# Lightning attention and MLP on one core: the first two windows opened tile by tile

## The chip, the cores and the metric

The kernel runs on one core of one Trainium2 chip. Its engines work side by side, each through its own list of instructions in the order written: TensorE (PE) multiplies, VectorE (DVE), ScalarE (ACT) and GpSimd (POOL) do elementwise work, SyncE (SP) issues transfers; ACT and POOL issue some too. The metric is the device time of one execution in microseconds; the runs of the kernel before took 214.71, 215.11 and 215.28 us, the median is 215.11.

## The reference

Inputs are q, k, v of shape 4 (batch) x 8 (heads) x 768 (tokens) x 64, and a decay lam per head.

```python
Dmask = np.where(rel >= 0, lam[:, None, None] ** rel[None, :, :], 0.0)
for b in range(nb):                       # blocks of 64 tokens
    intra = np.einsum('bhic,bhjc->bhij', qb, kb) * Dmask[None]
    intra = np.einsum('bhij,bhjd->bhid', intra, vb)
    inter = np.einsum('bhid,bhde->bhie', qb * lam_pow[None], kv_state)
    out[:, :, sl] = intra + inter
    kv_state = lam_block[None, :, None, None] * kv_state + np.einsum('bhsd,bhse->bhde', kb_dec, vb)
...
xn = (x - mu) / np.sqrt(var + 1e-06) * g_ln
ch = np.maximum(xn @ w_ch1, 0.0) @ w_ch2
return (x + ch).astype(np.float32)
```

So: causal linear attention with an exponential decay and a running K·V state, heads put side by side to 512 columns, then a normalised two-layer MLP (512 to 2048 to 512) with a residual.

## The kernel before

**Tiling.** The 4 x 768 tokens are 12 windows of 256 tokens; window u belongs to batch u mod 4. A window has two tiles of 128 tokens ("ab" 0 and 1). In the first six windows a load puts two neighbouring tokens on each partition, so tile 0 lies on partitions 0 to 63 and tile 1 on 64 to 127, with all 8 heads along the row (`source`, `load_window`). Decay is folded into q (`lam_q`) and v (`lam_v`) as powers of lam, so a 0/1 mask remains for the scores.

**Steps of a window.** `in_k`, `in_q`, `in_v` (lines 195 to 216) cast to bf16 and scale; `transpose_pe` transposes k and q on PE and copies the result out of PSUM (later windows use a DMA transpose); `scores` and `mask` form the masked scores; `kv` and `new_state` form the state; `av` and `inter` accumulate the output in PSUM (`po`); `norm` takes mean and variance on DVE and writes the centred, scaled rows `xc`; `to_xT` transposes them for the MLP. `reader` is a small DVE copy between the two passes of `inter`, which write the same PSUM.

**The MLP.** W1 and W2 are loaded and cast by POOL-issued transfers in four pieces each (`load_w1`, `load_w2`). `m1` computes 512 hidden values for both tiles of a window at a time, `m1.tile(c, i)` one W1 piece c for one tile i; ACT applies Relu into `hT`. `m2(i, part)` multiplies `hT` by W2 in four parts, `finish` scales, adds the residual and stores.

**What sets the order.** Everything is under `tc.manual_schedule()`: each engine runs its instructions in the order in which the program text calls the steps. The opening (lines 588 to 695) is written out by hand for windows 0 and 1; `m1a`, `m1b` are their first MLP halves. From line 831 on, `plan` is a list of MLP units, and `add(at, ...)` hangs attention steps of later windows behind entry `at`. `behind(x)` lets POOL read one value of x, so that what POOL issues next waits until x has landed. `load_window(u, after_pool=True)` has POOL write one value into the new buffer first, so SP's loads wait for POOL. PSUM tiles of the tag `mm` rotate over four buffers; scores have two, and `po` two.

Of the kernel before, what the change touches and what calls it, by code (L numbers as in the profile page):

```python
# [16 lines left out]
def kernel(  # L17
# [76 lines left out]

    w1 = [const.tile([128, KA, DF // NWC], BF16, name=f"w1_{c}") for c in range(NWC)]
# [9 lines left out]

    lam_b = const.tile([128, H], F32)
    nc.scalar.dma_start(lam_b, lam[None, :].to_broadcast([128, H]))
    load_window(0, parts=2)
    g_row = const.tile([128, DM], F32)
    g_one = const.tile([1, DM], F32)  # L110
    nc.scalar.dma_start(g_one, moe_g_ln[None, :])

# [39 lines left out]
    nc.vector.tensor_scalar(e_q[half[1]], e_q[half[1]], float(-C), None, op0=ALU.add)  # L152
    e_v = const.tile([128, 2], F32)
# [11 lines left out]

    lnlam = const.tile([128, H], F32)
    nc.scalar.activation(lnlam, lam_b, ACT.Ln)
    lam_q = const.tile([128, H, 2], F32)
    nc.scalar.activation(lam_q[:, :, 0], lnlam, ACT.Exp, scale=e_q)
# [296 lines left out]

    o_of = {}

    def mlp(g):
# [19 lines left out]
        def m1_tile(c, i):  # L489
# [4 lines left out]
            for b in range(W2K):  # L494
                for kk in range(KA):
# [92 lines left out]
    open_window(0)  # L588
    load_window(1)
    in_k(0, nc.vector, HA)  # L590
    transpose_pe(0, 0, (0, 1))
    keep_busy(1, "po0")
    for j in range(2):
        nc.scalar.activation(lam_v[:, :, j], lnlam, ACT.Exp, scale=e_v[:, j:j + 1])
    ln_p = lnlam.rearrange("p (a two) -> p a two", two=2)
    for e in range(2):
        nc.scalar.activation(lam_s[half[e]], ln_p[half[e], :, e], ACT.Exp, scale=float(C))
    nc.vector.tensor_tensor(lam_q[:, :, 1], lam_q[:, :, 0], lam_b, op=ALU.mult)
    nc.vector.tensor_copy(e_p[:, 0:1], io_p)
# [3 lines left out]
    in_q(0, nc.vector, HA)  # L603
    behind(qkv_in[0]["k"][:, 0, 0, 0:1])
    load_w1(0)
    in_k(0, nc.gpsimd, HB)
    in_q(0, nc.vector, HB)
    transpose_pe(0, 1, (0, 1))
    transpose_pe(0, 0, (2, 3), nc.vector)
    nc.scalar.copy(g_row, g_all)  # L610
    transpose_pe(0, 1, (2, 3))
    sqrt_first = const.tile([128, 1], F32)
    in_v(0, nc.gpsimd, HA)
    in_v(0, nc.gpsimd, HB)
    scores(0, 0)
    mask(0, 0)
    scores(0, 1, early=True)
    mask_by_act(0, 1)
    kv(0)
    new_state(0, 0, nc.scalar)  # L620
    av(0, (0, 1))
    av(0, (2, 3), (0,))
    av(0, (2, 3), (1,))
    inter(0, 0, fence=False)
    open_window(1)
    in_k(1, nc.scalar)
    norm(0, 0, early=True)
    reader(0)
    behind(qkv_in[1]["k"][:, 0, 0, 0:1])
    load_w1(1)  # L630
    load_w1(2)
    in_q(1, nc.gpsimd)
    load_w1(3)
    load_w2(0)
    in_v(1, nc.gpsimd)
    behind(w1[2][:, 0, 0:1])
    load_window(2, after_pool=True)
    m1a, m2a = mlp(0)
    m1b, m2b = mlp(1)

    def m1s(f, c, lo=0, hi=2):
        n = f.count // NWC
        for u in range(c * n + lo * n // 2, c * n + hi * n // 2):
            f(u)


    transpose_pe(1, 0, (0, 1), nc.vector)
    transpose_pe(1, 0, (2, 3), nc.vector)
    to_xT(0, 0)
    inter(0, 1)  # L650
    norm(0, 1, early=True)
    st[0]["tmp"] = state_sum(0, 1)
    m1a.tile(0, 0)
    to_xT(0, 1)
    transpose_pe(1, 1, (0, 1), nc.vector)
    transpose_pe(1, 1, (2, 3))
    m1a.tile(0, 1)
    keep_x(0, nc.vector.tensor_copy)
    nc.scalar.activation(sqrt_first, eps_t, ACT.Sqrt)
    scores(1, 0)  # L660
    scores(1, 1, early=True)
    mask(1, 0)
    mask(1, 1)
    m1s(m1a, 1, 0, 1)
    kv(1, "sc")
    new_state(1, 0, nc.scalar)
    m1s(m1a, 1, 1, 2)
    rstd_of(0)
    m1s(m1a, 2, 0, 1)
    av(1, (0, 1))  # L670
    av(1, (2, 3))
    inter(1, 0)
    norm(1, 0, early=True)
    m1s(m1a, 2, 1, 2)
    inter(1, 1)
    norm(1, 1, early=True)
# [250 lines left out]
```

## Time and profile before

| what | us |
|---|---|
| median of three runs | 215.11 (214.71 to 215.28) |
| the profiled execution, from first to last instruction | 214.9 |
| PE busy in it | 201.9 (94%) |
| DVE, ACT, POOL busy | 102.9, 87.1, 79.4 |
| first MLP tile starts on PE | 15.82 |
| first W2 product starts on PE | 37.68 |
| MLP of window 2 starts on PE | 55.02 |

A profile is one execution recorded by the hardware. Rows give start, length, engine, line, operation, output and inputs; a row with "x16" merges sixteen instructions. In brackets stands how long the engine was idle before, and what it had waited for. "PEld" is the load of the stationary operand. Matmuls are pipelined, so their merged rows may overlap. In a table of stretches each row is one stretch of time with the busy time of each engine, the granted TensorE clock, the busy share of the 16 DMA engines and the bytes moved. A "DMA" in a wait is a transfer that had not landed yet. "SPq", "ACTq" and "POOLq" rows are issues of transfers by the sequencers.

### The profile page before, as it was taken

Reading aid. Unit: us, or ns where it says so; the run is one execution under the profiler, and the core shown is the slowest. Engines: PE = TensorE matmul, PEld = TensorE weight load, DVE = VectorE, ACT = ScalarE, POOL = GpSimd, SP = SyncE. Lnnn points to the kernel's source line nnn. Section 1 sums busy time; section 2 is a strip of 40 time slices with the busy share of each in tenths; the row PEclk is TensorE's granted clock in tenths of the full one; section 3 lists DMA queues with packets and bytes.
Section 4 is the critical chain, followed back from the end, with each engine's and each line's share of the span. In section 5 each row is a group of like instructions: output and inputs, shape, how many; then the busy total and the mean of one; then the engine's idle time right before and its main releaser. Section 6 shows DMA issues by size and latency. Waiting matters only on the chain.

```text
span 214.9 us, 6642 instructions
## 1 busy us (share of the span) xinstructions
PE 201.9 (94%) x2884; PEld 138.2 (64%) x2899; DVE 102.9 (48%) x225; ACT 87.1 (41%) x165; POOL 79.4 (37%) x111
## 2 busy tenths in 40 slices
PE   2989999999799999999999999999999999999992
PEld 0568788454674675585585685784784874866861
DVE  3678461565168436747347256174183292522011
ACT  4765679120442244055063162261370460731600
POOL 4747139039464173229019138056065020000000
PEclk9999999999999999999999999999999999999998
DMA  4999999999999898799799999998998511320303
GB/s 130 289 272 207 219 263 160 236 284 234 215 303 208 169 229 153 110 215 209 126 220 199 137 230 200 177 203 198 206 246 131 128 27 27 99 52 0 98 3 95
DMA packets 94142, 37.13 MB, mean 173 GB/s; under 512 B 68385, under 2 KB 91169, under 8 KB 94114
## 3 DMA queue, kind: packets, MB, share of 16 engines
q1 hardware_dynamic: 89584, 32.38, 71.4%
q0 software_dynamic: 4224, 4.19, 12.4%
q8 instruction: 22, 0.36, 0.7%
q10 hardware_dynamic: 306, 0.14, 0.3%
q14 instruction: 6, 0.05, 0.1%
HBM read 27.27 MB, written 6.29 MB: 156 GB/s over the span
## 4 chain that ended last, share of the span: by engine, by line
PE 75%; DMA 13%; POOL 4%; SPq 3%; DVE 2%; issue 1%; POOLq 0%
PE pm L484 35%; PE pm L522 30%; DMA vin<-in_v_dram 6%; DMA qin<-in_q_dram 4%; SPq L71 3%; DMA kqT<-kq 2%; POOL kq L210 2%; POOL vb L216 2%; PE pm2h L513 2%; PE po L406 1%; PE po L393 1%; PE sc L247 1%; PE po L380 1%; PE sc L327 1%; PE pm1t L496 1%
## 5 line engine op out<-in xcount | busy, mean ns | idle before, releaser
L487 ACT ACTIVATE hT<-pm 128x512 bf16<-128x512 f32 x92 | 54.9, 601 | 91.2 <-PE pm L484 91.0
L484 PE MATMUL pm<-xT,w 128*128 128x256 bf16 x736 | 86.3, 273 | 1.9 <-DMA xT<-xc 1.2
L522 PE MATMUL pm<-w,hT 128*128 128x512 bf16 x353 | 81.1, 379 | 1.0 <-issue 0.3
L484 PEld LDWEIGHTS <-w 128*128 128x128 bf16 x736 | 69.8, 98 | 13.8 <-DMA xT<-xc 1.7
L522 PEld LDWEIGHTS <-hT 128*128 128x128 bf16 x368 | 35.5, 98 | 40.0
L543 DVE SCALAR_TENSOR_TENSOR o<-pm,rstd,x 128x512 f32<-128x512 f32 x23 | 17.1, 748 | 43.5 <-PE pm L522 43.4
L287 POOL TENSOR_TENSOR Sn<-Stmp,lam_s 128x256 bf16<-128x256 f32 x16 | 9.7, 611 | 69.7 <-DVE Stmp L365 49.0
L435 DVE SCALAR_TENSOR_TENSOR xc<-po,mv,g_row 128x512 bf16<-128x512 f32 (+1 forms) x24 | 16.8, 706 | 1.8
L257 DVE TENSOR_TENSOR mA<-sc,keep 128x512 bf16<-128x512 f32 x20 | 13.1, 685 | 6.8 <-PE sc L247 6.7
L428 ACT COPY x<-po 128x512 f32<-128x512 f32 x18 | 9.9, 588 | 11.3 <-PE po L393 5.3
L430 DVE BATCH_NORM_STATS2 stats<-x 128x6 f32<-128x512 f32 x18 | 12.4, 688 | 3.9 <-ACT x L428 3.9
L417 DVE COPY seen<-po 128x8 f32<-128x8 f32 x18 | 2.3, 162 | 23.2 <-PE po L406 23.2
L216 POOL TENSOR_TENSOR vb<-vin,lam_v 128x1024 bf16<-128x1024 f32 (+1 forms) x7 | 11.8, 1696 | 3.7 <-DMA vin<-in_v_dram 3.7
L210 POOL TENSOR_TENSOR kq<-qin,lam_q 128x512 bf16<-128x512 f32 x10 | 10.3, 1045 | 7.0 <-DMA qin<-in_q_dram 7.0
L210 POOL TENSOR_TENSOR kq<-qin,lam_p 128x512 bf16<-128x512 f32 x12 | 12.3, 1042 | 0.9 <-DMA qin<-in_q_dram 0.7
L216 POOL TENSOR_TENSOR vb<-vin,lam_p 128x1024 bf16<-128x1024 f32 x6 | 11.4, 1896 | 1.7 <-DMA vin<-in_v_dram 1.7
L199 POOL CAST kq<-kin 128x512 bf16<-128x512 f32 (+1 forms) x18 | 10.3, 599 | 0.6 <-DMA kin<-in_k_dram 0.6
L333 DVE TENSOR_TENSOR mA<-sc,keep 128x512 bf16<-128x512 f32 x12 | 8.2, 681 | 1.4 <-PE sc L327 1.4
L406 PE MATMUL po<-Sn,kqT 64*64 64x64 bf16 x216 | 7.4, 199 | 0.0
L224 PE MATMUL tp<-ident,kq 128*128 128x128 bf16 x48 | 6.2, 277 | 0.3 <-ACT kq L199 0.2
L406 PEld LDWEIGHTS <-kqT 64*64 64x64 bf16 x304 | 5.3, 108 | 1.5 <-issue 1.5
L224 PEld LDWEIGHTS <-kq 128*128 128x128 bf16 x48 | 4.1, 120 | 3.2 <-DVE kq L199 1.5
(98 smaller groups left out, 146.0 us busy)
## 6 DMA issues: line engine op xcount, KB each, us to landing
out_dram<-o SPq DMA_DIRECT2D x22, 256.0 KB, 4.5
w<-in_moe_w_ch_dram POOLq DMA_DIRECT2D x8, 512.0 KB, 9.6
kin<-in_k_dram SPq DMA_DIRECT2D x14, 256.0 KB, 3.9
qin<-in_q_dram SPq DMA_DIRECT2D x14, 256.0 KB, 5.2
vin<-in_v_dram SPq DMA_DIRECT2D x14, 256.0 KB, 5.6
kin<-in_k_dram SPq DMA_DIRECT2D x5, 512.0 KB, 6.5
qin<-in_q_dram SPq DMA_DIRECT2D x5, 512.0 KB, 8.7
vin<-in_v_dram SPq DMA_DIRECT2D x5, 512.0 KB, 7.7
```

The costliest lines, as they stand in the source:

```text
L199: (eng.copy if eng is nc.scalar else eng.tensor_copy)(dst[:, :, :, j], src[:, :, :, j])
L210: eng.tensor_tensor(dst[:, :, :, j], src[:, :, :, j], lq[:, :, :, j:j + 1].to_broadcast([128, n, 2, D]), op=ALU.mult)
L216: eng.tensor_tensor(st[u]["vb"][:, hs], qkv_in[u]["v"][:, hs], lv.to_broadcast([128, n, 2, D]), op=ALU.mult)
L224: nc.tensor.transpose(tp[:, i, j, :], s["kq"][:, a, p, j], ident)
L257: nc.vector.tensor_tensor(s[f"mA{hf}"][:, e], s[f"sc{hf}"][e], kp[:, None, :, :].to_broadcast([128, 2, 2, 128]), op=ALU.mult)
L406: nc.tensor.matmul(s["po"][ab][half[jq], 2 * p + e, :], lhsT=qT[half[e], p, jq, half[ab]], rhs=s["S"][ab][jq][half[e], p, :], start=False, ...
L430: nc.vector.bn_stats(stats, po if early else x)
L435: nc.vector.scalar_tensor_tensor(xc[:, sl], in0=po[:, sl], scalar=mv[:, 0:1], in1=g_row[:, sl], op0=ALU.subtract, op1=ALU.mult)
L484: nc.tensor.matmul(pm[:, b, :], lhsT=w1[n // W2K][:, kk, (n % W2K) * 128:(n % W2K + 1) * 128], rhs=xT_of[g][:, kk, 0:N], start=(b == 0 and ...
L487: nc.scalar.activation(hT[:, u * NB:(u + 1) * NB, 0:N], pm, ACT.Relu)
L522: nc.tensor.matmul(acc[i], lhsT=hT[:, kk, i * 128:(i + 1) * 128], rhs=w2[kk // W2K][:, kk % W2K, :], start=(kk == 0), stop=(kk == KB - 1))
L543: nc.vector.scalar_tensor_tensor(o[:, ab], in0=a, scalar=rstd[:, ab:ab + 1], in1=x[:, ab], op0=ALU.mult, op1=ALU.add)
```

## The change

Windows 0 and 1 are no longer loaded and worked on as windows of 256 tokens but as single tiles. In a tile the 128 tokens lie on 64 partitions, two to each, with heads 0 to 3 on partitions 0 to 63 and heads 4 to 7 on 64 to 127, so each tensor of a tile takes two transfers of 64 partitions. For window 0 SP issues one of the two and ACT the other; for window 1 SP issues all twelve. The `tile_*` functions do for one tile what the window functions do for two. ACT loads one table set for Ln and Exp at the start. The opening is rewritten: tile 0 goes through attention first; W1 piece 0 is issued behind the keys of window 0's tile 1, pieces 1 and 2 behind the keys of window 1's tiles, piece 3 behind POOL's work on window 1; W2 piece 0 waits for W1 piece 3. MLP tiles of window 1 are moved into the opening, and the remaining ones into the plan; steps of window 2 are hung one entry later; window 4 is loaded behind window 3's transposes. Inside `m1_tile` the loop over the contraction becomes the outer one.

```diff
+    def load_tiles(u, second=None):
...
+        for ab in range(2):
+            lo = cc * W + ab * C
+            for name in "kqv":
+                dst = got[name].rearrange("p (c h) x -> p c h x", c=2)
+                for hg in range(2):
+                    issue = lambda eng, hg=hg, ab=ab, dst=dst, x=src[name], lo=lo: eng.dma_start(
+                        dst[half[hg], ab], x[b, hg * 4:hg * 4 + 4, lo:lo + C, :].rearrange("h (p j) d -> p h (j d)", j=2))
+                    if hg == 1 and second is not None:
+                        second.append(issue)
+                    else:
+                        issue(nc.sync)
...
+    nc.scalar.preload_act_table_set("natural_log_exp_and_others")
     lam_b = const.tile([128, H], F32)
+    on_act = []
+    load_tiles(0, second=on_act)
+    on_act[0](nc.scalar)
     nc.scalar.dma_start(lam_b, lam[None, :].to_broadcast([128, H]))
-    load_window(0, parts=2)
+    on_act[1](nc.scalar)
...
+    for hg in range(2):
+        nc.scalar.activation(lnlam_t[half[hg]], lam_b[half[hg], hg * 4:hg * 4 + 4], ACT.Ln)
+    lam_tq = const.tile([128, 4, 2], F32)
+    nc.scalar.activation(lam_tq[:, :, 0], lnlam_t, ACT.Exp, scale=e_q)
+    nc.scalar.activation(lam_tq[:, :, 1], lnlam_t, ACT.Exp, scale=e_q1)
+    on_act[4](nc.scalar)
+    on_act[5](nc.scalar)
...
+    def tile_k(u, ab, eng):
+        src = qkv_in[u]["k"][:, ab]
+        dst = by_head(st[u]["kq"][:, ab, 0])
+        (eng.copy if eng is nc.scalar else eng.tensor_copy)(dst, src)
...
+    def tile_T(u, ab, i, copy):
+        s = st[u]
+        tp = mm_tile([128, 2, 2, 128], BF16, "tp")
+        for a in range(2):
+            for j in range(2):
+                nc.tensor.transpose(tp[:, a, j, :], s["kq"][:, ab, i, j, a], ident)
+        copy(s["kqT"][:, ab, i], tp)
...
+    def tile_mask_act(u, ab, e):
+        s = st[u]
+        m = s[f"mA{ab}"][:, e]
+        nc.scalar.copy(m, s[f"sc{ab}"][e])
+        kp = keep_h.rearrange("p a b t -> p a (b t)")
+        nc.vector.tensor_tensor(m, m, kp[:, None, :, :].to_broadcast([128, 2, 2, 128]), op=ALU.mult)
...
+    def tile_norm(u, ab):
...
+        for hg in range(2):
+            nc.vector.bn_stats(stats[:, hg], po[hg])
+        nc.vector.bn_aggr(mv, stats)
...
+    def tile_xT(u, ab):
...
+        for h, copy in enumerate((nc.scalar.copy, nc.vector.tensor_copy)):
+            xt = mm_tile([128, 2, 128], BF16, "xt")
+            for kk in range(2):
+                nc.tensor.transpose(xt[:, kk, :], s["xc"][:, ab, (2 * h + kk) * 128:(2 * h + kk + 1) * 128], ident)
+            copy(dst[:, 2 * h:2 * h + 2], xt)
...
-            for b in range(W2K):
-                for kk in range(KA):
+            for kk in range(KA):
+                for b in range(W2K):
...
+    load_tiles(1)
+    open_tiles(0)
+    tile_k(0, 0, nc.vector)
+    tile_T(0, 0, 0, nc.scalar.copy)
     keep_busy(1, "po0")
     for j in range(2):
+        nc.scalar.activation(lam_tv[:, :, j], lnlam_t, ACT.Exp, scale=e_v[:, j:j + 1])
+    tile_q(0, 0, nc.vector)
+    tile_T(0, 0, 1, nc.vector.tensor_copy)
+    tile_k(0, 1, nc.scalar)
+    nc.scalar.copy(g_row, g_all)
+    tile_v(0, 0, nc.gpsimd)
+    behind(qkv_in[0]["k"][:, 1, 0, 0, 0:1])
+    load_w1(0)
+    tile_q(0, 1, nc.gpsimd)
+    tile_v(0, 1, nc.gpsimd)
+    tile_scores(0, 0)
+    mask(0, 0, (0,))
+    tile_mask_act(0, 0, 1)
+    tile_T(0, 1, 0, nc.scalar.copy)
+    tile_av(0, 0, (0,))
+    tile_av(0, 0, (1,))
+    tile_T(0, 1, 1, nc.scalar.copy)
+    tile_kv(0, 0)
...
+    tile_state_first(0)
+    tile_norm(0, 0)
+    tile_scores(0, 1)
+    tile_xT(0, 0)
+    tile_keep_x(0, 0, nc.scalar.copy)
+    mask(0, 1)
+    m1a, m2a = mlp(0)
+    m1b, m2b = mlp(1)
+    tile_av(0, 1)
+    tile_inter(0, 0)
+    tile_inter(0, 1)
+    m1a.tile(0, 0)
+    open_tiles(1)
+    tile_k(1, 0, nc.scalar)
+    behind(qkv_in[1]["k"][:, 0, 0, 0, 0:1])
+    load_w1(1)
+    tile_norm(0, 1)
+    tile_v(1, 0, nc.gpsimd)
+    tile_T(1, 0, 0, nc.scalar.copy)
+    tile_xT(0, 1)
+    tile_q(1, 0, nc.vector)
+    m1a.tile(0, 1)
+    tile_keep_x(0, 1, nc.scalar.copy)
+    behind(qkv_in[1]["k"][:, 1, 0, 0, 0:1])
+    load_w1(2)
+    tile_T(1, 0, 1, nc.vector.tensor_copy)
+    m1a.tile(1, 0)
+    tile_scores(1, 0)
+    m1a.tile(1, 1)
+    tile_k(1, 1, nc.scalar)
+    tile_q(1, 1, nc.gpsimd)
+    tile_v(1, 1, nc.gpsimd)
+    load_w1(3)
+    mask(1, 0, (0,))
+    tile_mask_act(1, 0, 1)
+    tile_T(1, 1, 0, nc.scalar.copy)
+    tile_av(1, 0)
+    tile_kv(1, 0)
+    tile_norm(1, 0)
+    tile_T(1, 1, 1, nc.scalar.copy)
+    tile_state_first(1)
+    tile_scores(1, 1)
+    tile_kv(0, 1)
+    tile_xT(1, 0)
+    tile_keep_x(1, 0, nc.scalar.copy)
+    mask(1, 1)
+    m1b.tile(0, 0)
+    m1b.tile(1, 0)
+    tile_state_sum(0)
+    tile_av(1, 1)
+    tile_inter(1, 0)
+    tile_inter(1, 1)
+    m1a.tile(2, 0)
+    m1a.tile(2, 1)
+    tile_norm(1, 1)
+    behind(w1[2][:, 0, 0:1])
+    load_window(2, after_pool=True)
+    tile_state_second(0)
+    m1b.tile(2, 0)
+    tile_keep_x(1, 1, nc.scalar.copy)
+    tile_kv(1, 1)
+    tile_state_sum(1)
+    tile_xT(1, 1)
+    m1a.tile(3, 0)
+    behind(w1[3][:, 0, 0:1])
+    load_w2(0)
+    tile_state_second(1)
+    nc.scalar.activation(lam_q[:, :, 0], lnlam, ACT.Exp, scale=e_q)
...
     for i in range(2):
         nc.scalar.activation(lam_p[:, i], lnlam, ACT.Exp, scale=e_p[:, i:i + 1])
...
     nc.scalar.activation(sqrt_first, eps_t, ACT.Sqrt)
     rstd_of(0)
+    rstd_of(1)
     open_window(2)
     in_k(2, nc.vector)
     load_w2(1)
+    in_q(2, nc.gpsimd)
     load_w2(2)
+    in_v(2, nc.gpsimd)
     load_w2(3)
     load_window(3, after_pool=True)
-    load_window(4)
...
-    plan = [(m1b, n) for n in range(m1b.count // NWC, m1b.count)]
+    plan = [(m1a.tile, 3, 1), (m1b.tile, 3, 0)] + [(m1b.tile, c, 1) for c in range(NWC)]
...
-    add(2, (new_state, 0, 1, nc.gpsimd), (new_state, 1, 1, nc.gpsimd))
...
-    add(12, (s4, 2), (p4, 2), (p0, 3, nc.vector), (transpose_dma, 3))
+    add(13, (s4, 2), (p4, 2), (p0, 3, nc.vector), (transpose_dma, 3), (load_window, 4))
```

## The prediction

> **What bounds the kernel now.** I read the page first: PE 94% busy, TensorE's clock at 9 tenths throughout, so time is gained or lost only where PE waits or runs thin. The table of stretches, cut where PE's work changes, shows where (columns: stretch, length, then busy us of PE, PEld, DVE, ACT, POOL, clock, DMA share, GB/s):
>
> ```profile
> 0.00:15.80 15.80, 10.52 (x175) 6.44 (x176) 8.84 (x30) 9.79 (x23) 8.31 (x22) 1.00 0.95 229
> 15.80:20.77 4.97, 4.65 (x76) 4.33 (x75) 3.93 (x9) 2.48 (x5) 3.78 (x5) 1.00 1.24 212
> 20.77:37.68 16.91, 16.20 (x280) 13.82 (x281) 7.63 (x18) 13.51 (x27) 9.18 (x13) 1.00 1.12 213
> 37.68:55.02 17.34, 15.82 (x191) 7.38 (x193) 9.98 (x19) 2.06 (x4) 8.79 (x10) 1.00 1.12 250
> 55.02:214.90 159.88, 154.69 (x2165) 106.18 (x2176) 72.50 (x152) 59.24 (x107) 49.31 (x65) 1.00 0.77 153
> ```
>
> After 55.02 PE is the bound; the change touches only order there. The first 15.8 us fill the pipe; 20.77 to 37.68 is already dense; the DMA engines are full from about 4 us. PE's own timeline gives the anchors: the first MLP tile at 15.82 (cold: 1.86 us for 16 matmuls, 1.05 the second time), the wait for the second W1 piece at 20.77, the first W2 product at 37.68, the wait for window 2's xT at 55.02.
>
> ```profile
> 15.82 1.86 PE L496 MATMUL pm1t<-xT,w 128*128 128x128 bf16 x16 [0.32 <-ACT xT L456]
> 18.85 1.05 PE L496 MATMUL pm1t<-xT,w 128*128 128x128 bf16 x16
> 20.77 1.05 PE L484 MATMUL pm<-xT,w 128*128 128x256 bf16 x8 [0.30 <-DMA w<-in_moe_w_ch_dram]
> 55.02 1.25 PE L484 MATMUL pm<-xT,w 128*128 128x256 bf16 x10 [1.20 <-DMA xT<-xc]
> ```
>
> ACT's timeline shows one thing more: window 1's K cast runs at 12.46, long before PE is in the MLP. ACT works in written order, and this cast waits for no MLP tile.
>
> ```profile
> 12.46 1.17 ACT L199 CAST kq<-kin 128x512 bf16<-128x512 f32 x2
> 17.72 0.60 ACT L499 ACTIVATE hT<-pm1t 128x512 bf16<-128x512 f32 x1 [1.95 <-PE pm1t L496]
> ```
>
> **What the Trainium skill says.** "PSUM — Partial Sum Buffer", section "Engine vs sequencer instructions": ScalarE, VectorE and GpSimd queues are strict FIFO. The trace agrees: every ACT row stands in the order of the code. "DMA: Bandwidth & Descriptors", section "Issuing engines are not separate DMA queues": all issuers share the same 16 DMA engines, so a second issuer saves only issue time; here an SP issue takes 0.46 to 0.51 us while landings of 256 KB follow each other by about 0.9 us (K at 5.04 and 6.88, Q at 7.77, V at 8.77), so there is little to save. "ScalarE: Activation LUTs", section "Table sets: the hidden batching unit": Ln then Exp in one set needs one load; the trace loads twice before its Exp, 1.28 us each.
>
> **The change, part by part.** t0 is the start of the first MLP tile (15.82 now), M the first W2 product (37.68 now).
>
> *Up to t0.* Tile 0's K comes in two 128 KB DMAs, on SP and ACT. SP's half is issued as early as today; I take 5.1 for both (0 to +1.3 if ACT's sequencer waits out the table load). The lam DMA stands one issue (0.5) later: about 4.8. ACT: two Ln and two Exp at about 0.2 to 0.3 spacing to 5.8; two DMA issues (0.5 each) to 6.8; the kqT copy (L225, 0.58) to 7.3; two Exp (0.5) to 7.8. Only then can POOL scale V (L216, 1.04 for 128x512): 8.9. W1 piece 0 is issued behind it, not at 5.32 but at about 9: 0.2 for the read of K, 0.94 to issue. Then Q of tile 1 (1.04) to 11.1. PE transposes it (4, about 0.3), ACT copies (0.58), scores (0.64 at cold clock): 12.7. DVE meanwhile: norm of tile 0 from 10.4, two half-width statistics (estimate 0.38 each, half of the 0.69 row plus overhead; at most 0.69), 0.18, two L435 halves at 0.44: 12.2; xT's copy to 13.0; two masks (L257, 0.69): 14.4. The A·V product, S·Q, two 0.16 readers and the second S·Q: t0 not before 15.4. W1 piece 0 must have landed: W pieces take 7.4 to 11.0 us from issue, so 16.4 at the earliest. I take t0 = 16.5 (15.4 to 18.3): **+0.7**. The half-size loads and the saved table load (1.28) bring nothing here, because POOL's order and then DVE's take their place.
>
> *From t0 to M, work.* Equal: 16 MLP tiles at 0.9 (L496 x32 is 1.79 in the chain) = 14.4. Before, beside it: xT transposes 1.2, transposes of window 1's Q 0.5, scores 0.8, KV 0.45, A·V 0.82, S·Q 0.3, window 2's transposes 0.9 and scores 0.4: 19.8 with the MLP; 21.86 passed, so 2.1 were idle or cold. After, window 1's K transposes (0.5) move behind t0 too, and the KV of tile 1 of window 0 (0.2): 20.5, **+0.7**.
>
> *From t0 to M, new waits.* In the new order PE, ACT and DVE hand over in a ring with nothing for PE between. Prices: Relu 0.60, ACT cast 0.66, back-to-back spacing 0.5, ACT copy 0.58 (256 wide: 0.40, the skill's "ScalarE: Activation LUTs", section "What ACT_TABLE_LOAD costs", 186 ns plus 0.833 per element; the 512-wide row's 0.58 is close to its 0.61).
> (a) tile_k(1,0) stands on ACT behind the Relu of m1a.tile(0,0), and PE's next work is its transposes: Relu, cast, handover = 1.25 idle.
> (b) xT's ACT half waits behind the kqT copy, m1a.tile(0,1) behind it: 0.65.
> (c) tile_k(1,1) behind the Relu of m1a.tile(1,1), transposes next on PE: 1.25.
> (d) the ACT half of the mask behind that cast, then DVE's 0.46, before the odd heads' A·V: 0.45.
> (e) last transposes to copy (behind another) to scores(1,1): 0.65.
> (f) norm of tile (1,0), about 1.8 on DVE, to its xT: 0.25 after covers.
> (g) xT copy to m1b.tile(0,0): 0.45.
> (h) the two readers between the S·Q passes: 0.35.
> (i) five Exp (1.3), a table load (1.28) and three Sqrt (0.8) on ACT, now between the Relus of m1a.tile(3,0) and (3,1): 3.2 of ACT; four PSUM buffers hide some 2.0: 1.2. Before, the load at 20.55 hid under the wait for W1.
> Sum 6.5 against 2.1: **+4.4**. Below nothing is excluded for (a) and (c), which are pure dependence; the rest may overlap: 3.5 to 7.5 for the sum.
>
> W1 pieces 1 to 3 wait for later keys and POOL work, and come at about 20, 23 and 26.6; PE, delayed, uses them at 21.5, 31.7 and 35: hidden by the waits above; with those gone, piece 1 alone would hold PE to about 20. POOL now stands at tile_state_second for DVE's sums (about 30 and 34.5), and behind it W2 piece 0, piece 1, Q of window 2, W2 pieces 2 and 3 and window 3's load. W2 piece 0 issued near 31 lands at 38 to 41, M is 43.5: hidden, by 2 us. m1_tile's loop order and mask changes cost nothing: same counts.
>
> *After M.* The same 16.1 us of PE. window 4's load, which held SP until 48.98 in the profile while norm ended at 48.36 and kept the DMA engines full, goes behind xT(2) and kqT(3); xT's two transposes then start 0.6 earlier and land in about 4.5 instead of 5.9, but one plan entry (0.87) less lies between. The wait of 1.2 becomes 0.1 to 0.9, I take 0.5: **-0.7**. Window 4 lands some 10 us later; POOL reaches kq(4) at M+26, and today SP issues its transposes at M+25: hidden.
>
> Sum: 0.7 + 0.7 + 4.4 - 0.7 = +5.1 on the span of 214.9: **220.0 us** (M at 16.5 + 20.5 + 6.5 = 43.5). That span is 0.2 under the median of 215.11 and inside the runs' 214.71 to 215.28, so it needs no scaling. Within 0.3% (0.65 us) a measurement of this kernel can't tell from no change.
>
> **Rivals.**
> *Faster: the smaller first tile really opens PE early.* For it: DMA is full at the start, and half the bytes stand before tile 0's scores. It decides if t0 plus the waits falls below 18 us (16.5 plus 6.5 now): with t0 15.4 and waits of 1.0, M is 36.9, 0.8 earlier, then -0.7: 213.4. Against: POOL's and DVE's chains to 15.4, and (a), (c). Chance 0.12.
> *Half of it hides:* t0 15.4, waits 2.8: M 38.7, +1.0 less 0.7: about 215.2. Chance 0.08.
> *The second queue starts late:* K's ACT half behind the table load, 64-partition DMAs slower than 128-partition ones, which no row of before for loads shows; t0 18.3 instead of 16.5: 221.8. Chance 0.14.
> *A later wait:* two windows' loads share M+16 to M+30, and kqT(4) or xT(3) lands 1 to 2 late, where xT(3)'s consumer now starts with no slack (72.02 after 0.13 of issue): +1.5, 221.5. Chance 0.10.
> *My forecast:* 216 to 221.5: 0.56.
>
> **How the numbers follow.** Faster 0.12; same 0.08; slower 0.80, the last three. Below 215.0 lies about 0.14 (the fast case and part of the second), above 222.5 about 0.06: range 215.0 to 222.5.
>
> **What would show it.** First MLP tile at 16 to 17, not before 15.4; W1 piece 0 issued near 9; PE idle for over 1 us ahead of two four-transpose groups with ACT's cast as releaser; a table load on ACT past 33; first W2 product at 41.5 to 44.5; xT(2)'s wait under 1 us. Wrong if the first MLP tile stands before 14, or if the cast's groups show no idle PE.

## The result and the profile after

The changed kernel takes 236.63 us (median of four executions, 235.57 to 244.04) where the kernel before, run beside it, takes 215.19 (214.71 to 215.81): a ratio of 1.0958, 95% interval 1.089 to 1.1026. The longest execution ran at a lower TensorE clock; such executions are left out of this ratio and of all that follow. The direction was forecast, the size was not: +5 was written down and some +20 came. The profiled execution took 235.57 with a span of 233.8, so 18.9 of the span are to be explained.

The table of stretches of the kernel after, cut at the same four events as the table of before (columns: stretch, length, then busy us of PE, PEld, DVE, ACT, POOL, clock, DMA share, GB/s):

```profile
0.00:20.05 20.05, 9.12 (x151) 5.44 (x152) 8.16 (x26) 8.00 (x23) 10.09 (x23) 1.00 0.81 193
20.05:55.27 35.22, 26.28 (x477) 23.80 (x477) 13.60 (x36) 20.27 (x46) 10.63 (x16) 0.95 0.86 161
55.27:71.25 15.98, 15.72 (x197) 7.46 (x194) 9.55 (x19) 1.81 (x4) 4.48 (x4) 1.00 0.41 108
71.25:91.47 20.22, 16.48 (x241) 10.79 (x240) 9.09 (x18) 6.24 (x11) 11.38 (x15) 1.00 0.98 255
91.47:233.80 142.33, 137.73 (x1926) 95.38 (x1936) 63.96 (x135) 52.94 (x96) 41.72 (x54) 1.00 0.69 146
```

| stretch | before | after | difference | forecast |
|---|---|---|---|---|
| start to first MLP tile (t0) | 15.82 | 20.05 | +4.23 | +0.7 |
| t0 to first W2 product (M) | 21.86 | 35.22 | +13.36 | +5.1 |
| M to MLP of window 2 | 17.34 | 15.98 | -1.36 | -0.7 |
| MLP of window 2 to MLP of window 3 | 17.00 | 20.22 | +3.22 | 0 (a rival: +1.5) |
| the rest | 142.88 | 142.33 | -0.55 | 0 |

Between t0 and M, PE is idle for 8.94 (35.22 less 26.28 busy), against about 1.0 in the two stretches of before that cover it. It is also busy 5.4 longer, with 0.7 of moved work (eight transposes and sixteen K·V products): nearly all of the rest is matmuls that ran slower.

PE's timeline of the kernel before has these rows, of the first product and of the first MLP product of window 3 (start, length, then in brackets idle time and releaser):

```profile
4.12 2.04 PE L164 MATMUL g_all<-g_one,ones 1*128 1x512 f32 x2 [4.12 <-DMA g_one<-in_moe_g_ln_dram]
72.02 1.03 PE L484 MATMUL pm<-xT,w 128*128 128x256 bf16 x8
```

and that of the kernel after, a selection of rows:

```profile
7.04 2.04 PE L193 MATMUL g_all<-g_one,ones 1*128 1x512 f32 x2 [7.04 <-DMA g_one<-in_moe_g_ln_dram]
9.01 0.61 PE L533 MATMUL tp<-ident,kq 128*128 128x128 bf16 x4
20.05 1.89 PE L687 MATMUL pm1t<-xT,w 128*128 128x128 bf16 x16 [0.64 <-DMA w<-in_moe_w_ch_dram]
23.14 0.61 PE L533 MATMUL tp<-ident,kq 128*128 128x128 bf16 x4 [1.19 <-ACT kq L517]
24.69 1.87 PE L687 MATMUL pm1t<-xT,w 128*128 128x128 bf16 x16 [0.52 <-ACT xT L656]
28.85 1.07 PE L687 MATMUL pm1t<-xT,w 128*128 128x128 bf16 x16
31.11 0.40 PE L533 MATMUL tp<-ident,kq 128*128 128x128 bf16 x4 [1.20 <-ACT kq L517]
48.47 1.26 PE L260 MATMUL tp<-ident,kq 128*128 128x128 bf16 x8 [4.21 <-DVE kq L235]
49.52 3.23 PE L687 MATMUL pm1t<-xT,w 128*128 128x128 bf16 x32
...
91.47 1.03 PE L675 MATMUL pm<-xT,w 128*128 128x256 bf16 x8 [3.69 <-DMA xT<-xc]
```

Four things are to be seen. The first instruction on PE, the product that spreads the row g over the partitions, waits until 7.04, 2.92 later than before, and all else on PE stands behind it. The two waits for ACT's K cast are there, at 1.19 and 1.20. A wait of 4.21 stands ahead of window 2's transposes, and one of 3.69 for xT(3). And the first three MLP tiles of 16 matmuls take 1.8 to 1.9 (before, only the first did), against 1.07 later; 32 behind the long wait take 3.23, against 1.95 elsewhere.

Why W1 piece 0 comes late is on the timelines of ACT and POOL in the kernel after:

```profile
8.34 0.60 ACTq L109 DMA_DIRECT2D qin<-in_q_dram  x1
9.16 0.60 ACTq L109 DMA_DIRECT2D vin<-in_v_dram  x1
9.80 0.58 ACT L534 COPY kqT<-tp 128x512 bf16<-128x512 bf16 x1 [2.79 <-PE tp L533]
11.96 0.94 POOL L122 DMA_DIRECT2D w<-in_moe_w_ch_dram  x1
```

ACT's copy of the transposed K stands behind PE's transposes (done at 9.62) and behind two of ACT's own issues of transfers; ACT's Exp for `tile_v`, POOL's scaling of V and the issue of W1 piece 0 follow from it.

The cause of the 4.21 is on DVE's timeline, beside the same cast in the kernel before (L199):

```profile
30.20 0.95 DVE L199 CAST kq<-kin 128x512 bf16<-128x512 f32 x2 [0.85 <-DMA kin<-in_k_dram]
45.81 0.35 DVE L499 RECIPROCAL rstd<-std 128x2 f32<-128x2 f32 x2 [2.07 <-ACT std L497]
46.08 2.66 DVE L235 CAST kq<-kin 128x512 bf16<-128x512 f32 x2
```

and on POOL's of the kernel after in the same time:

```profile
45.38 0.80 POOL L125 DMA_DIRECT2D w<-in_moe_w_ch_dram  x1
46.20 1.91 POOL L252 TENSOR_TENSOR vb<-vin,lam_v 128x1024 bf16<-128x1024 f32 x1
48.05 1.00 POOL L125 DMA_DIRECT2D w<-in_moe_w_ch_dram  x1
```

The instructions of the cast's line (shortest, median and longest in ns; first and last start):

```profile
L235 DVE CAST kq<-kin x2: 414/1370/2327, 46.1 to 48.3; 128x512 bf16<-128x512 f32 x2
```

Window 2's K cast stands on DVE behind two reciprocals, and these behind ACT's five Exp, a table load and the Sqrt. When it comes at last, its first half takes 2.33 and its second 0.41; both together took 0.95 in the kernel before. The first half begins while POOL issues a W2 piece and ends 0.3 after POOL's scaling of V. The Trainium skill, "SBUF — State Buffer", section "Who interferes with whom", says that DVE and GpSimd share one pair of ports as an exclusive lock, and that casts and operations with two SBUF inputs can contend for it. The times agree with that in kind: the first half ends when POOL's scaling has ended. In every kernel of this study that leaves the cast at this place it takes 2.66 or 2.67 (eight profiles), and in the four that move it ahead of the block 0.90 to 1.20. So the place makes it slow; no run here tells the lock from another cause.

### The profile page after: what moved, and what is told of

Same layout as the page of the kernel before. It is cut to its first block, busy times and chain, and to the rows that moved or that the text cites. A ratio compares the mean times of both kernels' runs of the same rounds, so it can differ in the third digit from the quotient of the medians.

```text
span 233.8 us, 6892 instructions
## 1 busy us (share of the span) xinstructions
PE 205.3 (88%) x2981; PEld 142.9 (61%) x2995; DVE 104.4 (45%) x233; ACT 89.3 (38%) x179; POOL 78.3 (33%) x111
## 4 chain that ended last, share of the span: by engine, by line
PE 78%; DMA 10%; ACT 3%; issue 3%; DVE 2%; POOL 1%; SPq 1%; ACTq 0%; POOLq 0%; DVEq 0%
PE pm L713 31%; PE pm L675 30%; PE pm1t L687 7%; DMA vin<-in_v_dram 4%; DMA w<-in_moe_w_ch_dram 3%; PE pm2h L704 2%; DMA kin<-in_k_dram 1%; PE sc L283 1%; DVE kq L235 1%; PE po L442 1%; DMA xT<-xc 1%; PE po L416 1%; PE po L429 1%; POOL vb L252 1%; PE sc L363 1%
## 5 line engine op out<-in xcount | busy, mean ns | idle before, releaser
L678 ACT ACTIVATE hT<-pm 128x512 bf16<-128x512 f32 x80 | 47.9, 599 | 88.6 <-PE pm L675 88.5
L675 PE MATMUL pm<-xT,w 128*128 128x256 bf16 x640 | 74.0, 273 | 3.7 <-DMA xT<-xc 3.7
L675 PEld LDWEIGHTS <-w 128*128 128x128 bf16 x640 | 61.2, 98 | 13.8 <-issue 4.2
L687 PE MATMUL pm1t<-xT,w 128*128 128x128 bf16 x256 | 19.4, 245 | 1.2 <-DMA w<-in_moe_w_ch_dram 0.6
L687 PEld LDWEIGHTS <-w 128*128 128x128 bf16 x256 | 18.2, 112 | 1.8 <-issue 0.9
L690 ACT ACTIVATE hT<-pm1t 128x512 bf16<-128x512 f32 x16 | 9.4, 596 | 13.0 <-PE pm1t L687 13.0
L471 DVE SCALAR_TENSOR_TENSOR xc<-po,mv,g_row 128x512 bf16<-128x512 f32 x18 | 13.5, 751 | 1.6
L235 POOL CAST kq<-kin 128x512 bf16<-128x512 f32 x16 | 9.3, 612 | 10.0 <-PE pk L317 10.0
L246 POOL TENSOR_TENSOR kq<-qin,lam_q 128x512 bf16<-128x512 f32 x8 | 8.2, 1043 | 0.8 <-ACT lam_q L874 0.5
L252 POOL TENSOR_TENSOR vb<-vin,lam_v 128x1024 bf16<-128x1024 f32 x4 | 7.6, 1902 | 1.9 <-DMA vin<-in_v_dram 1.9
L193 PE MATMUL g_all<-g_one,ones 1*128 1x512 f32 x2 | 2.0, 1122 | 7.0 <-DMA g_one<-in_moe_g_ln_dram 7.0
```

Source lines behind the costliest of these rows:

```text
L235: (eng.copy if eng is nc.scalar else eng.tensor_copy)(dst[:, :, :, j], src[:, :, :, j])
L246: eng.tensor_tensor(dst[:, :, :, j], src[:, :, :, j], lq[:, :, :, j:j + 1].to_broadcast([128, n, 2, D]), op=ALU.mult)
L252: eng.tensor_tensor(st[u]["vb"][:, hs], qkv_in[u]["v"][:, hs], lv.to_broadcast([128, n, 2, D]), op=ALU.mult)
L471: nc.vector.scalar_tensor_tensor(xc[:, sl], in0=po[:, sl], scalar=mv[:, 0:1], in1=g_row[:, sl], op0=ALU.subtract, op1=ALU.mult)
L675: nc.tensor.matmul(pm[:, b, :], lhsT=w1[n // W2K][:, kk, (n % W2K) * 128:(n % W2K + 1) * 128], rhs=xT_of[g][:, kk, 0:N], start=(b == 0 and ...
L678: nc.scalar.activation(hT[:, u * NB:(u + 1) * NB, 0:N], pm, ACT.Relu)
```

## The experiments

All ratios are to the kernel before, timed beside the run; a time read from a timeline is that of one execution. Theory: a few accidents of order, each with its wait, make up what exceeds the forecast. Rivals: the waits hide one another, so that ending one only uncovers the next; or it is the slower matmuls that cost. The intervals of the edits made one at a time overlap that of the changed kernel (1.089 to 1.1026), so for these it is the wait in the timeline that tells, not the total.

**The row g first.** In the changed kernel, SP issues g ahead of all loads, where ACT had issued it as its fourth transfer.

```diff
+    nc.sync.dma_start(g_one, moe_g_ln[None, :])
     on_act = []
     load_tiles(0, second=on_act)
...
-    nc.scalar.dma_start(g_one, moe_g_ln[None, :])
```

> The changed kernel with one transfer moved: g_one is issued by SP ahead of everything instead of fourth on ACT. Order theory (PE's first instruction is the product with g_one, so all of PE's list stood behind that transfer until 9.01): the first transposes come at 6.6 instead of 9.01, W1 piece 0 is issued at about 9.6 instead of 11.96, the first MLP tile starts at about 17.6 instead of 20.05, the total falls by 2 to 3 us to about 234. Transfer theory (the opening is set by when q, v and W1 arrive): the transposes move, but the first MLP tile stays at 19.5 to 20 and the total within 1 us of 236.6.

Measured: 236.95 us, ratio 1.0941 [1.0839, 1.1043]. The first transposes come at 5.79 instead of 9.01, but W1 piece 0 is issued at 10.85 instead of 11.96 only, since ACT's copy (8.70) now stands behind ACT's issues alone; and the first MLP tile stands at 20.55. DVE's timeline of this run shows what took the place of the wait:

```profile
11.17 3.68 DVE L556 TENSOR_TENSOR mA<-mA,keep_h 128x512 bf16<-128x512 bf16 x1 [0.46 <-ACT mA L554]
```

The mask's second half, a product of two SBUF operands, takes 3.68 here and 0.42 in the kernel after. POOL scales Q and V and issues W1 without a pause from 9.74 on in this run; the product begins inside an issue of W1 (10.85 to 11.79) and ends at 14.85, just after the next such issue (to 14.74). So the gain at the head was paid back whole, in another place. It is not plain that g's place brought this on: at the same point of the same issue the product took 0.42 in the kernel after and in the two runs that follow.

**Window 2's K cast first.** In the changed kernel, the cast goes ahead of the Exp, table and Sqrt block.

```diff
     tile_state_second(1)
+    open_window(2)
+    in_k(2, nc.vector)
     nc.scalar.activation(lam_q[:, :, 0], lnlam, ACT.Exp, scale=e_q)
...
-    open_window(2)
-    in_k(2, nc.vector)
     load_w2(1)
```

> The changed kernel with one step moved: window 2's K cast on DVE stands ahead of the Exp, table load and Sqrt block instead of behind it. Order theory (DVE's cast was queued behind a reciprocal that waited for ACT's block): PE's 4.2 us wait before window 2's transposes goes, with the cold clock after it, the first W2 product comes 4.5 to 6 us earlier (49.5 to 51 instead of 55.27), total about 231. Contention theory (the cast itself was slow, 2.66 us for two, because POOL worked beside it): it stays slow, and only 1.5 to 2.5 us are won.

Measured: 233.41 us, ratio 1.0834 [1.0748, 1.0921], span 231.6. DVE's timeline of this run:

```profile
43.36 0.90 DVE L235 CAST kq<-kin 128x512 bf16<-128x512 f32 x2
```

and PE's behind it:

```profile
45.63 0.61 PE L260 MATMUL tp<-ident,kq 128*128 128x128 bf16 x8
46.08 1.06 PE L687 MATMUL pm1t<-xT,w 128*128 128x128 bf16 x16
48.04 1.05 PE L687 MATMUL pm1t<-xT,w 128*128 128x128 bf16 x16 [0.91 <-ACT hT L690]
```

The 4.21 and the slow cast are gone, and t0 to M shrinks by 5.0 (35.22 to 30.25). What is left of the step is the wait of 0.91 for a Relu. Of the 5.0 only 2.2 reach the end of the span: t0 was 1.4 later in this execution, and xT(3) again waits, 3.87, with slower matmuls behind it.

**Window 4's load early.** In the changed kernel, the load goes back to where it was, behind window 3's.

```diff
     load_window(3, after_pool=True)
+    load_window(4)
...
-    add(13, (s4, 2), (p4, 2), (p0, 3, nc.vector), (transpose_dma, 3), (load_window, 4))
+    add(13, (s4, 2), (p4, 2), (p0, 3, nc.vector), (transpose_dma, 3))
```

> The changed kernel with window 4's load put back where it was before, directly behind window 3's. Queue theory (SP's list is too full at M+16 to M+32, so window 3's xT transpose is issued late): the 3.7 us wait for xT at 91.47 goes, xT of window 2 costs up to 1.2 again, net 2.0 to 3.5 us faster, about 233.5. If the wait comes from the denser W2 phase alone, it stays above 2.5 us and the total moves by less than 1.

Measured: 233.9 us, ratio 1.0833 [1.0717, 1.095], span 230.1. M stays at 55.27; xT(2) doesn't wait either way; xT(3)'s wait is gone. PE's timeline of this run:

```profile
83.68 4.05 PE L713 MATMUL pm<-w,hT 128*128 128x512 bf16 x18
87.68 1.03 PE L675 MATMUL pm<-xT,w 128*128 128x256 bf16 x8
```

The span is 3.7 shorter, the 3.69 of the wait. SP's own timeline of the kernel after says why: it issues without a break from 70.89 on, and xT(3) stands at the end.

```profile
80.39 0.67 SPq L71 DMA_DIRECT2D vin<-in_v_dram  x1
81.16 2.14 SPq L741 DMA_DIRECT2D out_dram<-o  x2
83.47 4.01 SPq L267 DMA_TRANSPOSE kqT<-kq  x2
87.59 2.51 SPq L487 DMA_TRANSPOSE xT<-xc  x2
```

**Window 1's K casts early.** In the changed kernel, both casts go on ACT ahead of the Relu that they stood behind.

```diff
-    m1a.tile(0, 0)
     open_tiles(1)
     tile_k(1, 0, nc.scalar)
+    m1a.tile(0, 0)
...
+    tile_k(1, 1, nc.scalar)
     m1a.tile(0, 1)
...
     m1a.tile(1, 1)
-    tile_k(1, 1, nc.scalar)
```

> The changed kernel with the two ACT casts of window 1's K moved ahead of the Relus they stood behind (ahead of the first MLP tile, and ahead of m1a.tile(0,1)). Order theory: the two waits of 1.2 us before the four-transpose groups go and the MLP tiles run warm sooner; first W2 product 2 to 4 us earlier, total about 233.5. Transfer theory: W1 piece 1 or 2 or window 1's Q then holds PE instead, less than 1 us is won.

Measured: 237.3 us, ratio 1.099 [1.0907, 1.1074], span 234.6. Both waits of 1.2 for the casts are gone (one of 1.15 for the mask stands in the place of the second), and t0 to M is 3.5 shorter (31.7), since the second and third MLP tiles run at 1.05 too. But t0 is 21.76: the mask's product took 3.44 in this run, and PE waited 3.40 for it. No net gain; the theory's mechanism holds, its total doesn't.

**The mask out of PSUM.** To take the cause of that product away: g first, and DVE masks both halves out of PSUM, as the change itself does for tile 1 of both windows, with no ACT copy and no product of two SBUF operands.

```diff
-    mask(0, 0, (0,))
-    tile_mask_act(0, 0, 1)
+    mask(0, 0)
```

> The changed kernel with the row g issued first by SP, and tile 0's second mask half taken by DVE out of PSUM instead of by an ACT copy and a DVE product of two SBUF operands (the product that took 3.68 us beside POOL's Q, V and W1 issue). Theory A (VectorE locked out by POOL's SBUF work): no DVE row ahead of the first A.V over 1.2 us, PE's wait of 3.6 us near 15 gone, the first MLP tile set by W1 piece 0 alone (issue 10.9 plus 7.4 to 8: 18.3 to 18.9), M (first W2 product) about 53, total about 234. Rival B (the lock is an accident of the waits' order and DVE was late anyway): PE still waits over 2 us for DVE or ACT before the first A.V, first MLP tile over 20.

Measured: 236.63 us, ratio 1.0818 [1.0698, 1.0937]. No long DVE row is left ahead of the first A·V product (1.29 for both halves), the wait of 3.64 is gone and t0 is 18.35, inside the 18.3 to 18.9 of theory A. M, however, is 54.57 and not 53, in a profiled execution of 237.19; and the total is not told apart from that of the changed kernel.

**ACT's late halves on SP.** As the run before, with window 0's last two halves issued by SP.

```diff
-    on_act[4](nc.scalar)
-    on_act[5](nc.scalar)
+    on_act[4](nc.sync)
+    on_act[5](nc.sync)
```

> As the run before, and window 0's last two ACT-issued halves (Q and V of tile 1) issued by SP. Theory A (ACT's own issues hold its copies, and through them POOL and W1): the K/Q copy on ACT at 6.5 to 7 instead of 8.7, W1 piece 0 issued near 8.7 instead of 10.9, first MLP tile at 16.5 to 17.5, total about 232. Rival B (the issue slots are the bound, whoever issues): SP's last load of windows 0 and 1 stands 1.2 us later, tile 1's work and the first MLP tile stay within 0.5 us of the run before.

Measured: 234.01 us, ratio 1.0745 [1.0652, 1.0838]. Timelines of ACT, POOL and PE in this run:

```profile
6.43 0.58 ACT L534 COPY kqT<-tp 128x512 bf16<-128x512 bf16 x1 [0.47 <-PE tp L533]
8.59 0.94 POOL L122 DMA_DIRECT2D w<-in_moe_w_ch_dram  x1
88.29 1.86 PE L675 MATMUL pm<-xT,w 128*128 128x256 bf16 x8 [4.32 <-DMA xT<-xc]
91.09 2.89 PE L675 MATMUL pm<-xT,w 128*128 128x256 bf16 x16
```

ACT's first copy of transposed K comes at 6.43 (9.80 in the kernel after), W1 piece 0 is issued at 8.59, t0 is 16.04 and M 51.51: theory A in the opening, a little better than forecast. The total gives back part. xT(3) now waits 4.32, and the 8 and 16 matmuls behind the wait take 1.86 and 2.89 instead of 1.03 and 1.92, 1.8 more; from 85 to 95 us the profile lists a granted clock of 0.63 and 0.69, where the kernel after has 1.00.

**All repairs.** g first, mask out of PSUM, SP for the late halves, window 1's casts and window 2's cast early, window 4's load early.

> All repairs together in the changed kernel: g first, the mask out of PSUM, all of ACT's late halves on SP, window 1's two K casts on ACT ahead of the Relus, window 2's K cast on DVE ahead of the Exp, table and Sqrt block, window 4's load behind window 3's. Theory A (the loss is a chain of named order effects: opening 3.5, window 2's cast 5.0, the casts of window 1 3.5, window 4 3.7): their sum is 15.7 of the 20.3 lost, M at 42 to 45, no wait over 1.5 for xT(3), total 219 to 224, still slower than the kernel before since the ring of hand-overs stays. Rival B (the effects overlap: with one wait gone another engine is the bound, as the first run with g showed): M at 46 or more and total 225 to 230. Rival C (only order was lost): 217 or less.

Measured: 222.07 us, ratio 1.023 [1.0149, 1.0311]; t0 17.37, M 45.62, xT(2) waits 1.28, xT(3) not at all. Theory A, with M 0.6 over its bound. Alone, g, the casts and window 4's load changed the span by between -3.7 and +0.8; all together by -11.9 (233.8 to 221.9). They don't add up: in the two runs in which the opening was repaired alone, the slow mask product took the gain.

**Window 4's load late, in the kernel before.**

```diff
-    load_window(4)
...
-    add(12, (s4, 2), (p4, 2), (p0, 3, nc.vector), (transpose_dma, 3))
+    add(12, (s4, 2), (p4, 2), (p0, 3, nc.vector), (transpose_dma, 3), (load_window, 4))
```

> The kernel before with one edit of the change alone: window 4's load moved behind window 3's transposes in the plan. Theory A (moved there, the 3 loads and the loads of window 5 behind them hold SP's queue over window 3's xT transposes whatever the opening was): xT(3) waits 2.5 to 3.7 us, less 0.7 to 1.2 for xT(2) whose wait goes: 1.5 to 2.8 slower, 216.6 to 218. Rival B (it costs only in the changed opening, where the plan's later steps are denser): xT(3) does not wait, total 0.7 to 1.2 faster.

Measured: 221.96 us, ratio 1.023 [1.0154, 1.0306]. PE's timeline of this run:

```profile
74.94 1.86 PE L484 MATMUL pm<-xT,w 128*128 128x256 bf16 x8 [4.29 <-DMA xT<-xc]
...
77.73 2.83 PE L484 MATMUL pm<-xT,w 128*128 128x256 bf16 x16
```

xT(2)'s wait of 1.20 is gone, as forecast, and xT(3) waits 4.29, with the first 24 matmuls behind it taking 4.69 instead of 2.95. Theory A in kind, at about twice its size. This edit, which the prediction booked as a small gain, costs by itself about what the prediction gave the whole change.

**The row g late, in the kernel before.** SP issues g behind window 0's six loads, where ACT had issued it as its second transfer.

```diff
-    nc.scalar.dma_start(g_one, moe_g_ln[None, :])
+    nc.sync.dma_start(g_one, moe_g_ln[None, :])
```

> The kernel before with one edit: the row g issued by SP behind window 0's six loads instead of by ACT as its second transfer. Theory A (PE's first instruction, the g product, holds everything behind it until g lands): g lands near 8, the first transposes at about 10 instead of 6.1, and the first MLP tile 2.5 to 4 us later, total 2.5 to 4 slower. Rival B (the opening has slack there, as the first run with g in the changed kernel suggests, where 3.2 us at the head gave nothing): first MLP tile within 1 us of 15.8, total within 1 us.

Measured: 223.4 us, ratio 1.0274 [1.0176, 1.0373]. PE's timeline of this run:

```profile
9.16 2.04 PE L164 MATMUL g_all<-g_one,ones 1*128 1x512 f32 x2 [9.16 <-DMA g_one<-in_moe_g_ln_dram]
...
20.20 1.11 PE L393 MATMUL po<-vb,mA 64*64 64x64 bf16 x32 [3.55 <-DVE mA L268]
```

g lands 5.04 later than before and the first MLP tile comes 8.24 later, at 24.06: theory A, and more. The additional wait of 3.55 is again for a mask product of two SBUF operands (4.12 for two, against 0.92 in the kernel before), which again begins inside an issue of W1 by POOL. So the head of PE's queue costs here, though the run doesn't part the 5.04 of g from the slow product; and that product isn't special to the changed kernel.

**Another order on SP, in the kernel before.** Window 4's load late, and its K/Q transposes moved behind xT(3).

```diff
-    add(25, (transpose_dma, 4))
...
-    add(30, (s4, 3), (p4, 3))
+    add(30, (s4, 3), (p4, 3), (transpose_dma, 4))
```

> The kernel before with window 4's load behind window 3's transposes, and window 4's K/Q transposes moved from plan entry 25 to entry 30, behind xT(3). Theory A (xT(3) was late only because SP issues in order and kqT(4), needed 12 us later, stood ahead of it): xT(2) and xT(3) both wait under 0.3, total 0.5 to 1.3 faster than before. Rival B (the transfers themselves, window 4's and 5's, hold xT(3), in whatever order SP issues): xT(3) still waits 2 us or more, total 2 to 4 slower.

Measured: 218.93 us (median of sixteen executions), ratio 1.0123 [1.0085, 1.0161]: slower by 1.2%. PE's timeline of this run:

```profile
73.38 1.05 PE L484 MATMUL pm<-xT,w 128*128 128x256 bf16 x8 [1.14 <-DMA xT<-xc]
...
75.64 0.42 PE L247 MATMUL sc<-kqT 64*64 64x128 bf16 x16 [0.83 <-DMA kqT<-kq]
```

The order does matter (xT(3) waits 1.14 instead of 4.29), but the premise was wrong: window 4's K and Q aren't needed 12 us later, their scores come 1.2 us behind xT(3). With window 4's load ahead of them, neither order had both in time. It is neither theory A nor rival B. Another part of the loss, a wait of 2.46 for POOL's V at 24.63, lies ahead of anything that the edit touches; 0.4 of it is in the profile of before. Why it varies stays open, and since it is most of the 2.6 lost, the total says little of the order.

**The same order with all repairs.** As the run with all repairs, but window 4's load as the change has it, and the transposes behind xT(3).

> All repairs of the earlier run, but with window 4's load left where the change puts it and its K/Q transposes behind xT(3) instead. Theory A (as for the kernel before): xT(2) does not wait (1.28 with window 4 early), xT(3) waits under 0.5; total about 1 us under the run with all repairs, 220.5 to 221.5 where that took 222.1, still 3.5 to 5 over the kernel before. Rival B: xT(3) waits 2 us or more and the total is 223 or more.

Measured: 224.56 us, ratio 1.0387 [1.0329, 1.0446]. xT(2) doesn't wait, xT(3) waits 0.67 and window 4's K/Q 0.88. Rival B in the total, neither in the waits; the early load is better.

**Idle matmuls in a short wait.** g first, mask out of PSUM and ACT's halves on SP; and two idle matmuls in one of the waits of 1.2.

```diff
+    keep_busy(2, "sc")
     tile_T(1, 0, 0, nc.scalar.copy)
```

> The changed kernel with g first, mask out of PSUM and window 0's last ACT halves on SP, and two idle matmuls (1.26 us) on PE in the wait of 1.20 us ahead of window 1's first transposes. Theory A (the wait makes the MLP tiles behind it run at half rate): the second and third MLP tiles take about 1.05 each instead of 1.86 and 1.91, the next MLP tiles come 1 to 1.7 us earlier. Rival B (the rate has another cause): both stay at 1.8 or more, and the fill costs 0 to 0.2.

Measured: one execution of 230.01 us, the one profiled, and three of 234.51 to 234.99, which are left out, so no ratio is given. In the timeline the tiles behind the wait take 1.05 and 1.06, as theory A has it. But the next run has the same fill, and there they take 1.87 and 1.68. So whether a short wait slows the tiles behind it isn't settled by this.

**Idle matmuls in the long waits.** As above, with 16 in the wait for window 2's cast and 14 in the wait for xT(3).

```diff
-    add(1, (transpose_pe, 2, 0, (0, 1, 2, 3)))
+    add(1, (keep_busy, 16, "sc"), (transpose_pe, 2, 0, (0, 1, 2, 3)))
...
+    add(starts[3] - 1, (keep_busy, 14, "sc"))
```

> The run with two idle matmuls ahead of window 1's first transposes, and besides 16 idle matmuls (3.5 us at full clock) in the wait of 4.2 us ahead of window 2's K transposes, and 14 (3.0) in the wait of 3.5 us for xT(3). All the waits themselves stay. Theory A[...]: the MLP tiles behind window 2's transposes take 1.95 for 32 matmuls instead of 3.2 to 3.6, the clock stays at 1.00 from 40 to 60 us, executions lie closer together, and the median is 229 to 231. Rival B (the clock's dips are unconnected with the waits): dips remain in these places, the median stays at 233 to 235.

Measured: 229.83 us (228.27 to 231.41), ratio 1.064 [1.0585, 1.0695]. PE's timeline of this run:

```profile
40.34 3.62 PE L777 MATMUL idle<-keep_h,ident 128*128 128x512 bf16 x16
44.72 0.90 PE L260 MATMUL tp<-ident,kq 128*128 128x128 bf16 x8 [0.77 <-DVE kq L235]
45.46 1.95 PE L687 MATMUL pm1t<-xT,w 128*128 128x128 bf16 x32
...
82.22 3.19 PE L777 MATMUL idle<-keep_h,ident 128*128 128x512 bf16 x14
85.49 1.03 PE L675 MATMUL pm<-xT,w 128*128 128x256 bf16 x8
```

DVE's cast and xT(3) are as late as ever, PE only does something useless meanwhile, and the 32 matmuls take 1.95 instead of 3.23 to 3.62. Theory A in the timeline: without the idle stretches the matmuls behind them run at full rate, though nothing else came earlier. In the total, against the run with ACT's late halves on SP, it is worth 2.3 (from the ratios 1.0745 and 1.064, whose intervals overlap) to 4.2 (from the medians); the short fill is part of that difference.

**All repairs, and idle matmuls in short waits.**

> All repairs, and idle matmuls in the shorter waits of the opening (two ahead of the first MLP tile, two ahead of the second, three ahead of the last scores of window 1). Theory A: the second MLP tile takes 1.05 instead of 1.43 to 1.86 and the 32 matmuls at 28.9 take 1.95 instead of 3.29, no dip of the clock below 0.9 before the first W2 product, M at 43.5 to 44.5 instead of 45.6, total 220 to 221 where all repairs took 222.1. Rival B: M stays at 45 or more, total 222 or more.

Measured: 221.77 us, ratio 1.0261 [1.0216, 1.0307]. t0 17.11, M 44.33, no slow tile but the first, all as theory A has it in the trace; the total is not told apart from all repairs alone. No kernel of this study beats the one before. What is left of the loss lies from t0 to M, 27.22 against 21.86 in the kernel before: PE is idle there for 3.11 against 1.02, and busy 3.3 longer, of it 1.6 with idle matmuls and 0.7 with moved work.

## Why the prediction was wrong

The direction and the ring of hand-overs were right. (a) and (c) were priced at 1.25 each and measured 1.19 and 1.20; (b) 0.65, measured 0.52; (d) 0.45, measured 0.30; (e) 0.65, measured 0.67; (h) 0.35, measured 0.34; ahead of the products of (f) and (g) PE shows no wait. xT(2)'s wait went.

From t0 to M, 13.4 was added where 5.1 was forecast. PE's idle time grew by 7.9 against 4.4 for the waits, and what is left of the excess, 4.7, is matmuls that ran slower, which the sum had at nothing. In the kernel with all repairs and idle matmuls, t0 is 17.11 and M 44.33, where the forecast had 16.5 and 43.5, and the loss is 5.6 us (2.61%) where it had 5.1. That agreement is in part luck: (a) and (c), 2.5 of the forecast, no longer stand in that kernel, and other waits and work take their room. Five steps of the prediction failed.

*"ACT: two Ln and two Exp … two DMA issues … the kqT copy … to 7.3".* This step followed ACT's list, but not where g stands in it: fourth instead of second, and PE's first instruction needs g. g landed at 7.04, and lam, taken at "about 4.8", at 6.08; the copy came at 9.80, W1 piece 0 was issued at 11.96 instead of "near 9", t0 was 20.05. With g first, the mask out of PSUM and ACT free of its late issues, the same steps gave 6.43, 8.59 and 16.04: the working fits a queue that the change didn't have. Tile 0's keys were not what was late: their cast began at 4.11, against 5.04 before and the 5.1 that the prediction took. So the smaller loads did bring the first keys sooner, the rival "the second queue starts late" is not what happened, and nothing stood ready to use them. "Two DMA issues (0.5 each)" was too little also: in window 0 a transfer of 128 KB over 64 partitions took 0.60 to 0.77 to issue, more than one of 256 KB over 128 before (0.46 to 0.51), so two halves cost 1.2 or more where one whole cost 0.5. ACT's own copy then stood behind two such issues, which began only at 8.34 and 9.16 though the Exp ahead of them ended at 7.02. What delayed them no run shows.

*(i), "four PSUM buffers hide some 2.0: 1.2".* For the Relus the price was about right (0.91 when only that wait was left). What it missed is DVE: its next instruction for PE, window 2's cast, stands behind the reciprocals that wait for this block. The prediction named who waits for ACT on PE, and not who waits for it on DVE. The term measured 4.21 of PE idle; moving the cast took 5.0 out of t0 to M. Of it 1.7 is the slow cast itself (2.66 against 0.95), which the prediction had not considered.

*"Window 4 lands some 10 us later … hidden" and "-0.7".* The gain came, -1.36, and was overpaid: +3.22 at window 3. The rival "a later wait" had the place, with 1 to 2 for the delay; it was 3.69, and 4.29 in the kernel before. The word that failed is "hidden": it was worked out for kqT(4) alone, and not for what stands behind the load on SP. The load now stands ahead of window 5's loads, two outputs, kqT(4) and xT(3), and xT(3)'s transposes were issued 4.6 later (87.59 against 82.97 with the load early). That xT(3) has no slack was seen, and should have decided it.

*The unit of a wait.* All waits were summed at their length. Behind the long waits the matmuls ran at about half rate for several us. The Trainium skill, "TensorE: Matmul & The Clock Gate", section "What's actually happening", gives about 3.4 us without work as the time after which the array falls back to half rate, in a window that runs free of the kernel. For single waits behind the opening the timelines of all runs agree: slower matmuls stood behind each of nine waits of 4.21 to 4.32, behind three of five of 3.51 to 3.87 (not behind the 3.69 of the kernel after), and not behind one of 3.13. But the length of one wait isn't all: in the two runs with all repairs and no idle matmuls the 32 matmuls at 28.90 took 3.29 and 3.42 behind several pauses, the longest of them 1.15, and with idle matmuls in some of these 1.95.

*DVE's slow instructions.* No term of the sum was for them. In the kernel after it is the cast alone; in two of the first four experiments it was the mask's product too (3.68 and 3.44 instead of 0.42), and that set t0 there. Why it is slow stays open.

The signs to look for did their part: the table load on ACT past 33 (at 44.09), idle PE ahead of two transpose groups with ACT's cast as releaser, and xT(2)'s wait under 1 us were all there; the first MLP tile, the issue of W1 piece 0 and M were outside what was written, which is where the sum broke.

## What to carry to other kernels

When an issue list is rewritten, write down for each engine the first instruction that waits and the place of its transfer in the new list; a row of 2 KB in fourth place instead of second held the whole of PE for three us. When an engine is blocked for a moment, ask what else in the *next* engine's queue stands behind the one that waits for it, and beside which work of other engines it will then run: a cast moved by such a block took 2.66 here instead of 0.95. And price a wait of PE of four us with the slow matmuls behind it too: here they took 1.3 to 2 us more, and idle matmuls in two such waits may be worth 2 to 4 us in the total, while ending the waits and the other order effects was worth some 15.

## What was not expected of the hardware

- The same DVE product of two bf16 SBUF operands, 128x512, took 0.42 or 3.44 to 3.78, and half a cast 0.41 or 2.33. All the long ones (the product in two runs of the changed kernel with an edit and in the kernel before with g late, the cast in the kernel after and in the seven runs that leave it there) began inside an issue of a weight piece by POOL, with POOL's scaling of Q or V straight behind it, and ended during POOL's next issue or within 0.2 of its end. But in the kernel after and in two other runs the product began inside such an issue as well (at 12.32 in the kernel after, the issue from 11.96 to 12.90) and took 0.42. What decides is open.
- The granted clock as the profile lists it is 1.00 over the first 24 us of every run, while the first tile of 16 matmuls takes 1.86 to 1.91 there and later ones 1.05. For the opening the durations must be read, not the clock.
